# Second product accumulated on the first in one PSUM bank, one VectorE sum per block

## The chip, the cores and the metric

The kernel runs on one core of one Trainium2 chip. The metric is the device time of one execution in microseconds (us). Three runs of the kernel before gave 288.61, 289.20 and 290.28; their median is 289.2. A difference is told in us or in per cent of that median.

## What is computed

A WaveNet layer: a causal convolution of three taps with dilation 2, then tanh of one half of the channels times sigmoid of the other half, then a matrix product. `x` is 2 x 16000 x 256, `w` is 3 x 256 x 512, `w_o` is 256 x 256, all bf16.

```python
xp = jnp.pad(x, ((0, 0), (pad, 0), (0, 0)))          # pad = (K - 1) * dil = 4
h = jnp.einsum('btc,cd->btd', xp[:, pad:pad + T, :], w[0])
for i in range(1, K):
    off = pad - i * dil
    h = h + jnp.einsum('btc,cd->btd', xp[:, off:off + T, :], w[i])
z = jnp.tanh(h[..., :D]) * _sigmoid(h[..., D:])
return z @ w_o
```

So `h[t] = x[t] w0 + x[t-2] w1 + x[t-4] w2`.

## The kernel before

**Layout.** Time is split as t = 4r + j. The input arrives transposed in SBUF (tile `xt`: channels on the partitions, then j, channel half, r), by DMA transposes of the sync queue, except for the first 160 rows, which come as they are and are transposed on TensorE (`turn`). A group is 256 rows r (1024 time steps); each of the two sequences has 16 groups, the very first and the very last of 160 rows. 32 groups make 128 blocks: each group has four blocks, one for each 128 of the 512 columns of `h` (in the order 0, 2, 1, 3, so that a tanh block is followed by its sigmoid block).

**Two halves of time.** With xc = x at j = 0, 1, yc = x at j = 2, 3 and xp, yp the same one row earlier, a block needs

- for j = 0, 1: xc w0 + yp w1 + xp w2
- for j = 2, 3: yc w0 + xc w1 + yp w2

Done directly (`direct`, the first four blocks) this is 12 matmuls, six for each half (three taps, two channel halves). The other 124 blocks use four products in place of six, that is 8 matmuls of 512 columns (`products(k, which)`, L208 to L227):

- product 2: (xc - yp) times wm, wm = (w0 + w2 - w1) / 2
- product 1: (xc + yp) times wp, wp = (w0 + w2 + w1) / 2
- product 3: (yc - yp) times w0
- product 0: (xp - xc) times w2

Product 1 plus product 2 plus product 0 is the half j = 0, 1; product 1 minus product 2 plus product 3 is the half j = 2, 3.

**Before the change** product 2 goes into a PSUM bank "b" and product 1 into a bank "a". ScalarE copies b into SBUF (`copy_m2`, L254, tile `ss`). VectorE makes both sums in place (`combine`, L261: b = a - ss; L262: a = a + ss). Product 3 is then accumulated on b and product 0 on a, and ScalarE applies tanh or sigmoid to b and to a (`activate`, L275). VectorE multiplies tanh and sigmoid (`gate`, L284, tile `zz`); TensorE multiplies by w_o (`out_mm`, L295, four matmuls of 256 columns in a piece, four pieces in a group); ScalarE copies a piece to SBUF (`out_evict`, L309) and the sync queue stores it.

**Moving operands.** `m` = xc - yp (`pre_m`, L183) and `p` = xc + yp (`pre_p`, L189) are made by VectorE, the differences `d` of products 3 and 0 (`pre_d`, L200) by GpSimd, each a group ahead; for group 1 three of the four d's are VectorE's. The weights wm and wp are made by VectorE at the start (`weights`, L149 to L152).

**PSUM.** Eight banks: pool `ps_a` has three buffers, `ps_b` three, `ps_o` two. A buffer that is asked for anew waits for the last reader of its tile three allocations earlier (two for `ps_o`).

**Order.** The schedule is written by hand; each engine runs its instructions in the order of the program text. After the start the main loop has one step per block k:

- TensorE: products 2 and 1 of block k, products 3 and 0 of block k-1, one piece of output matmuls
- ScalarE: copy of block k, eviction of the last piece, activations of block k-1 (b, then a)
- VectorE: one of pre_m, gate, pre_p, gate; then the two sums of block k
- GpSimd: one d for the next group, held behind VectorE's operation

The start: a few warm-up matmuls on zeros (`warm_up`, L97) write into tiles of `ps_a`; then TensorE transposes and runs the direct blocks 0 and 1, tap by tap, then 2 and 3, with products 2 and 1 of block 4 set before the last tap of block 3. Meanwhile VectorE makes the weights, the first gate, m, p and three d's.

Of the kernel before, what the change touches and what calls it, by code (L numbers as in the profile page):

```python
# [9 lines left out]
ALU = mybir.AluOpType  # L10
# [3 lines left out]
def kernel(  # L14
# [18 lines left out]
    nc = tc.nc  # L33
    bf16 = mybir.dt.bfloat16
    f32 = mybir.dt.float32
    B, T, D = x.shape
    K, _, D2 = w.shape
    P = 128
    assert K == 3 and D % P == 0 and D2 == 2 * D and T % 64 == 0
    CT = D // P  # L40
    NT = D // P
    RH = 16
    RG = 256
# [5 lines left out]
    N_DIRECT = 4  # L49
# [15 lines left out]
    for b in range(B):  # L65
# [4 lines left out]
        while i < len(rs):  # L70
            n = cuts.pop(0) if cuts else 2
# [17 lines left out]
    ps_a = ctx.enter_context(tc.tile_pool(name="ps_a", bufs=3, space=bass.MemoryType.PSUM))  # L89
    ps_b = ctx.enter_context(tc.tile_pool(name="ps_b", bufs=3, space=bass.MemoryType.PSUM))  # L90
# [1 line left out]
    ctx.enter_context(tc.manual_schedule())  # L92

    def warm_up(n):
        wps = ps_a.tile([P, 2 * RG], f32, name="a")
        for _ in range(n):
            nc.tensor.matmul(  # L97
                wps[:], lhsT=warm[:, 0:P], rhs=warm[:, :],
                start=True, stop=True,
            )  # L100
# [24 lines left out]
    w_taps = [w0_sb, w12_sb[:, 0], w12_sb[:, 1]]  # L125
    nc.scalar.preload_act_table(ACT.Sigmoid)
    warm_up(N_WARM_A)
    xns = []
    for i, (r0, r) in enumerate(TILES):
        xn = consts.tile([P, 4, D], bf16, name=f"xn{i}")  # L130
        nc.sync.dma_start(
            out=xn[:r], in_=x[0, 4 * r0:4 * (r0 + r), :].rearrange("(r j) c -> r j c", j=4)
# [12 lines left out]
    wp_sb = consts.tile([P, CT, D2], bf16)  # L145
# [27 lines left out]
    def views(g):  # L173
        G = groups[g]
        xt, c, R = xts[G["chunk"]], RH + G["col"], G["R"]
        return (xt[:, 0:2, :, c - 1:c - 1 + R], xt[:, 2:4, :, c - 1:c - 1 + R],
                xt[:, 0:2, :, c:c + R], xt[:, 2:4, :, c:c + R])

    def pre_m(g):
        xp, yp, xc, yc = views(g)  # L180
        G = groups[g]
        G["m"] = m_pool.tile([P, 2, CT, RG], bf16, name="mm")
        return nc.vector.tensor_tensor(out=G["m"][:, :, :, :G["R"]], in0=xc, in1=yp, op=ALU.subtract)  # L183
# [7 lines left out]
    def pre_d(g, part, eng, behind=None):  # L191
        xp, yp, xc, yc = views(g)
        G = groups[g]
        R = G["R"]
        if "d" not in G:
            G["d"] = d_pool.tile([P, 4, CT, RG], bf16, name="dd")
        h, q = divmod(part, 2)
        a, s = (yc, yp) if h == 0 else (xp, xc)
        j = 2 + q if h == 0 else q
        ins = eng.tensor_tensor(out=G["d"][:, j, :, :R], in0=a[:, q], in1=s[:, q], op=ALU.subtract)  # L200
        if behind is not None:
            tc.add_manual_dep(
                ins.ins, behind.ins.name,
                mybir.DependencyInfo(mybir.DependencyClass.Sync, mybir.DependencyReason.DATA),
                reason="GpSimd reads SBUF while VectorE's sums read PSUM",
            )

    def products(k, which):  # L208
        g, oi = divmod(k, 4)
        G = groups[g]  # L210
        o = O_ORDER[oi]
        osl = slice(o * P, (o + 1) * P)
        R = G["R"]
        N = 2 * R
        if which in (1, 2):
            G["ab"[which - 1], oi] = (ps_a, ps_b)[which - 1].tile([P, 2 * RG], f32, name="ab"[which - 1])
        wmat, mv, bank, first = {
            2: (wm_sb, lambda ct: G["m"][:, :, ct, :R], "b", True),
            1: (wp_sb, lambda ct: G["p"][:, :, ct, :R], "a", True),
            3: (w_taps[0], lambda ct: G["d"][:, 2:4, ct, :R], "b", False),  # L220
            0: (w_taps[2], lambda ct: G["d"][:, 0:2, ct, :R], "a", False),
        }[which]
        for ct in range(CT):
            nc.tensor.matmul(  # L224
                G[bank, oi][:, :N], lhsT=wmat[:, ct, osl], rhs=mv(ct),
                start=first and ct == 0, stop=ct == CT - 1, skip_group_check=True,
            )  # L227

    def direct(k, taps):

        g, oi = divmod(k, 4)
        G = groups[g]
        o = O_ORDER[oi]
        osl = slice(o * P, (o + 1) * P)
        R = G["R"]
        xp, yp, xc, yc = views(g)
        for tap in taps:
            if tap == 0:
                G["a", oi] = ps_a.tile([P, 2 * RG], f32, name="a")
                G["b", oi] = ps_b.tile([P, 2 * RG], f32, name="b")  # L240
            for bank, mv in (("a", (xc, yp, xp)[tap]), ("b", (yc, xc, yp)[tap])):
                for ct in range(CT):
                    nc.tensor.matmul(  # L243
                        G[bank, oi][:, :2 * R], lhsT=w_taps[tap][:, ct, osl], rhs=mv[:, :, ct, :],
                        start=tap == 0 and ct == 0, stop=tap == K - 1 and ct == CT - 1,
                        skip_group_check=True,
                    )

    def copy_m2(k):
        g, oi = divmod(k, 4)  # L250
        G = groups[g]
        N = 2 * G["R"]
        G["ss", oi] = ss_pool.tile([P, 2 * RG], f32, name="ss")
        nc.scalar.copy(out=G["ss", oi][:, :N], in_=G["b", oi][:, :N])  # L254

    def combine(k):
        g, oi = divmod(k, 4)
        G = groups[g]
        N = 2 * G["R"]
        pa, pb, ss = G["a", oi], G["b", oi], G["ss", oi]  # L260
        nc.vector.tensor_tensor(out=pb[:, :N], in0=pa[:, :N], in1=ss[:, :N], op=ALU.subtract)  # L261
        nc.vector.tensor_tensor(out=pa[:, :N], in0=pa[:, :N], in1=ss[:, :N], op=ALU.add)  # L262

    def activate(k):
        g, oi = divmod(k, 4)
        G = groups[g]
        R = G["R"]
        o = O_ORDER[oi]
        if oi == 0:
            G["th"] = act_pool.tile([P, NT, 4, RG], bf16, name="th")  # L270
            G["sg"] = act_pool.tile([P, NT, 4, RG], bf16, name="sg")
            G["z"] = z_pool.tile([P, NT, 4, RG], bf16, name="zz")
        dst = G["th"][:, o] if o < NT else G["sg"][:, o - NT]
        for h, bank in ((1, "b"), (0, "a")):
            nc.scalar.activation(  # L275
                out=dst[:, 2 * h:2 * h + 2, :R],
                in_=G[bank, oi][:, :2 * R].rearrange("p (q r) -> p q r", q=2),
                func=ACT.Tanh if o < NT else ACT.Sigmoid,
            )

    def gate(g, dt):
        G = groups[g]
        R = G["R"]
        return nc.vector.tensor_tensor(  # L284
            out=G["z"][:, dt, :, :R], in0=G["th"][:, dt, :, :R], in1=G["sg"][:, dt, :, :R], op=ALU.mult
        )
# [30 lines left out]
    NG = len(groups)  # L317
    NB = 4 * NG
    todo, made = [], []
    turn(0)  # L320
    turn(1)
    warm_up(N_WARM_B)
    for tap in range(K):
        for k in range(2):
            direct(k, (tap,))
    weights()
    for k in range(2):
        activate(k)
# [5 lines left out]
    for part in range(3):  # L334
        last = pre_d(1, part, nc.vector)
    pre_d(1, 3, nc.gpsimd, last)

    direct(3, range(K - 1))
    products(N_DIRECT, 2)
    products(N_DIRECT, 1)  # L340
    copy_m2(N_DIRECT)
    direct(3, (K - 1,))
    activate(3)
    combine(N_DIRECT)
    pre_d(2, 0, nc.gpsimd, pre_m(2))

    k = N_DIRECT + 1
    while k < NB + 2 or todo or made:
        g, oi = divmod(k, 4)
        if k < NB:  # L350
            products(k, 2)
            products(k, 1)
            copy_m2(k)
        if k <= NB:
            products(k - 1, 3)
            products(k - 1, 0)

        for piece in made:
            out_evict(*piece, False)
        made = []  # L360
        n = 1 if k < NB else 2
        while todo and todo[0][0] <= k and n:
            piece = todo.pop(0)[1]
            out_mm(*piece)
            made.append(piece)
            n -= 1

        last = None
        if k < NB and oi in (0, 2) and g + 1 < NG:
            last = (pre_m if oi == 0 else pre_p)(g + 1)  # L370
        if oi == 3 and g < NG:
            last = gate(g, 0)
        if oi == 1 and 1 <= g <= NG:
            last = gate(g - 1, 1)
            G = groups[g - 1]
            for rb0 in range(0, G["R"], P):
                for jp in range(2):
                    todo.append((k + 1, (g - 1, rb0, jp)))
        if k < NB and g + 1 < NG:
            pre_d(g + 1, oi, nc.gpsimd, last)  # L380
        if k < NB:
            combine(k)
        if k <= NB:
            activate(k - 1)

        if k < NB and oi == 3 and loaded < len(chunks) and groups[min(g + 1, NG - 1)]["chunk"] + 2 >= loaded:
            load_chunk(loaded)
            loaded += 1
        k += 1
# [30 lines left out]
```

## Time and profile before

| | |
|---|---|
| three runs | 288.61, 289.20, 290.28 us (median 289.2) |
| span of the profiled execution, first to last instruction | 286.7 us |
| own time of the profiled execution | not listed; the median of the runs is 2.5 us above its span |
| granted TensorE clock, mean | 1.000 |
| TensorE matmuls (PE) | 280.3 us busy, 98% |
| TensorE weight loads (PEld) | 152.8 us, 53% |
| VectorE (DVE) | 245.2 us, 86% |
| ScalarE (ACT) | 261.0 us, 91% |
| GpSimd (POOL) | 126.3 us, 44% |
| VectorE sums, L261 and L262 | 124 each, mean 693 and 683 ns |
| ScalarE copy of product 2, L254 | 124, mean 580 ns |
| ScalarE activations, L275 | 256, mean 606 to 608 ns |
| ScalarE eviction, L309 | 128, mean 593 ns |

Busy time is the union of an engine's instructions; instructions that follow each other can overlap in the records, so the sum of their lengths can be larger than the busy time. Matmul ends are modelled: a matmul of 512 columns shows 377 ns on average, while the next one of a stream starts sooner than that. Rows of a timeline give the start from the beginning of the span, the length, the engine (an engine name with a q is its sequencer), the line, the operation, out<-in, the shape and the count of merged instructions; in brackets the idle time before it and what ended it.

### The profile page before, as it was taken

The numbers are of one execution on the slowest core, as the hardware profiler recorded it, in microseconds if no ns is written. First come the engines' busy times: TensorE is split into PE (matmuls) and PEld (weight loads), VectorE is DVE, ScalarE is ACT, GpSimd is POOL, SyncE is SP. The second block draws the span as 40 slices with busy tenths as digits, with TensorE's granted clock in tenths as the row PEclk, the third lists the DMA queues.
The fourth block names the chain that finished last, engine by engine and source line by source line (L and its number), as shares of the span: only waits on it lengthen the run. The fifth ranks groups of instructions, "written<-read, shape, count | busy, mean of one in ns | idle before, by whom it ended". The sixth has DMA issues, their size and how long they took to land.

```text
span 286.7 us, 4706 instructions
## 1 busy us (share of the span) xinstructions
PE 280.3 (98%) x1577; PEld 152.8 (53%) x1577; DVE 245.2 (86%) x384; ACT 261.0 (91%) x511; POOL 126.3 (44%) x129
## 2 busy tenths in 40 slices
PE   7999999999999999999999999999999999999994
PEld 3644555555555555555555555555555555555572
DVE  1998888898898988988988988988988988988860
ACT  2388999999999999999999999999999999999995
POOL 1254444454445445445445445445445545445300
PEclk9999999999999999999999999999999999999999
DMA  8991793561826427181361915428272351211213
GB/s 201 201 153 46 187 169 107 129 159 41 220 75 140 123 81 178 73 215 48 112 188 39 224 74 134 129 70 190 77 178 83 107 158 44 75 58 53 75 73 119
DMA packets 75463, 34.47 MB, mean 120 GB/s; under 512 B 66256, under 2 KB 67280, under 8 KB 75440
## 3 DMA queue, kind: packets, MB, share of 16 engines
q1 hardware_dynamic: 74640, 33.40, 44.7%
q10 hardware_dynamic: 800, 0.79, 0.9%
q8 instruction: 12, 0.20, 0.3%
q14 instruction: 11, 0.09, 0.1%
HBM read 1.25 MB, written 16.38 MB: 61 GB/s over the span
## 4 chain that ended last, share of the span: by engine, by line
PE 91%; DVE 3%; DMA 2%; ACT 2%; issue 0%; ACTq 0%
PE b L224 36%; PE a L224 36%; PE o_ps L295 19%; DMA w_sb<-in_w_dram 2%; ACT osb L309 1%; DVE zz L284 1%; DVE b L261 0%; DVE mm L183 0%; DVE wm_sb L152 0%; DVE wt_sb L150 0%; DVE wp_sb L152 0%; ACT sg L275 0%; DVE dd L200 0%; ACT th L275 0%; DVE pp L189 0%
## 5 line engine op out<-in xcount | busy, mean ns | idle before, releaser
L200 POOL TENSOR_TENSOR dd<-xt 128x512 bf16<-128x512 bf16 (+1 forms) x121 | 125.4, 1037 | 145.4 <-DVE zz L284 79.2
L261 DVE TENSOR_TENSOR b<-a,ss 128x512 f32<-128x512 f32 (+1 forms) x124 | 85.9, 693 | 17.2 <-ACT ss L254 16.5
L262 DVE TENSOR_TENSOR a<-a,ss 128x512 f32<-128x512 f32 (+1 forms) x124 | 84.7, 683 | 0.0
L254 ACT COPY ss<-b 128x512 f32<-128x512 f32 (+1 forms) x124 | 72.0, 580 | 13.7 <-PE b L224 1.7
L224 PEld LDWEIGHTS <-w_sb 128*128 128x128 bf16 x496 | 48.5, 98 | 57.9 <-issue 1.3
L295 PE MATMUL o_ps<-wo_sb,zz 128*128 128x256 bf16 (+1 forms) x512 | 76.5, 273 | 0.7 <-ACT osb L309 0.7
L309 ACT CAST osb<-o_ps 128x512 bf16<-128x512 f32 (+1 forms) x128 | 75.5, 593 | 0.5 <-ACT osb L309 0.5
L224 PE MATMUL b<-mm,wm_sb 128*128 128x512 bf16 (+1 forms) x248 | 73.2, 377 | 0.1
L224 PE MATMUL b<-dd,w_sb 128*128 128x512 bf16 (+1 forms) x248 | 73.1, 377 | 0.1
L224 PE MATMUL a<-pp,wp_sb 128*128 128x512 bf16 (+1 forms) x248 | 73.2, 377 | 0.0
L224 PE MATMUL a<-dd,w_sb 128*128 128x512 bf16 (+1 forms) x248 | 73.2, 377 | 0.0
L295 PEld LDWEIGHTS <-zz 128*128 128x128 bf16 (+1 forms) x512 | 49.8, 98 | 33.0 <-PE b L224 0.8
L284 DVE TENSOR_TENSOR zz<-th,sg 128x1024 bf16<-128x1024 bf16 (+1 forms) x64 | 44.3, 691 | 12.6 <-ACT sg L275 12.4
L275 ACT ACTIVATE th<-b 128x512 bf16<-128x512 f32 (+1 forms) x64 | 38.8, 606 | 3.8 <-PE b L243 3.7
L275 ACT ACTIVATE sg<-b 128x512 bf16<-128x512 f32 (+1 forms) x64 | 38.9, 607 | 1.0 <-PE b L243 0.6
L224 PEld LDWEIGHTS <-wp_sb 128*128 128x128 bf16 x248 | 24.2, 98 | 28.9 <-DVE pp L189 0.5
L275 ACT ACTIVATE sg<-a 128x512 bf16<-128x512 f32 (+1 forms) x64 | 38.9, 608 | 0.0
L275 ACT ACTIVATE th<-a 128x512 bf16<-128x512 f32 (+1 forms) x64 | 38.8, 606 | 0.0
L224 PEld LDWEIGHTS <-wm_sb 128*128 128x128 bf16 x248 | 24.0, 98 | 3.9 <-DVE mm L183 0.5
L189 DVE TENSOR_TENSOR pp<-xt 128x1024 bf16<-128x1024 bf16 (+1 forms) x31 | 21.8, 702 | 0.0
L183 DVE TENSOR_TENSOR mm<-xt 128x1024 bf16<-128x1024 bf16 (+1 forms) x31 | 21.1, 680 | 0.0
L243 PEld LDWEIGHTS <-w_sb 128*128 128x128 bf16 x48 | 4.7, 97 | 2.2
(22 smaller groups left out, 26.0 us busy)
## 6 DMA issues: line engine op xcount, KB each, us to landing
out_dram<-osb SPq DMA_DIRECT2D x62, 256.0 KB, 2.0
w_sb<-in_w_dram ACTq DMA_DIRECT2D x1, 512.0 KB, 5.5
xn<-in_x_dram SPq DMA_DIRECT2D x2, 160.0 KB, 3.7
w_sb<-in_w_dram ACTq DMA_DIRECT2D x1, 256.0 KB, 4.0
xt<-in_x_dram SPq DMA_TRANSPOSE x16, 6.5
wo_sb<-in_w_o_dram SPq DMA_DIRECT2D x1, 128.0 KB, 5.5
out_dram<-osb SPq DMA_DIRECT2D x2, 64.0 KB, 1.6
```

The lines of the kernel that those rows point to most:

```text
L183: return nc.vector.tensor_tensor(out=G["m"][:, :, :, :G["R"]], in0=xc, in1=yp, op=ALU.subtract)
L189: return nc.vector.tensor_tensor(out=G["p"][:, :, :, :G["R"]], in0=xc, in1=yp, op=ALU.add)
L200: ins = eng.tensor_tensor(out=G["d"][:, j, :, :R], in0=a[:, q], in1=s[:, q], op=ALU.subtract)
L224: nc.tensor.matmul(G[bank, oi][:, :N], lhsT=wmat[:, ct, osl], rhs=mv(ct), start=first and ct == 0, stop=ct == CT - 1, skip_group_check=True,)
L243: nc.tensor.matmul(G[bank, oi][:, :2 * R], lhsT=w_taps[tap][:, ct, osl], rhs=mv[:, :, ct, :], start=tap == 0 and ct == 0, stop=tap == K - ...
L254: nc.scalar.copy(out=G["ss", oi][:, :N], in_=G["b", oi][:, :N])
L261: nc.vector.tensor_tensor(out=pb[:, :N], in0=pa[:, :N], in1=ss[:, :N], op=ALU.subtract)
L262: nc.vector.tensor_tensor(out=pa[:, :N], in0=pa[:, :N], in1=ss[:, :N], op=ALU.add)
L275: nc.scalar.activation(out=dst[:, 2 * h:2 * h + 2, :R], in_=G[bank, oi][:, :2 * R].rearrange("p (q r) -> p q r", q=2), func=ACT.Tanh if o ...
L284: return nc.vector.tensor_tensor(out=G["z"][:, dt, :, :R], in0=G["th"][:, dt, :, :R], in1=G["sg"][:, dt, :, :R], op=ALU.mult)
L295: nc.tensor.matmul(o_ps[:rn, q, :], lhsT=G["z"][:, dt, 2 * jp + q, rb0:rb0 + rn], rhs=wo_sb[:, dt, :], start=(dt == 0), stop=(dt == NT - 1),)
L309: nc.scalar.copy(out=osb[:rn, 2 * jp:2 * jp + 2, :], in_=o_ps[:rn])
```

## The change

Product 1 is accumulated on top of product 2 in bank b, after ScalarE has copied product 2 out of it. Bank b then holds the sum of the two. One VectorE instruction (`scalar_tensor_tensor`) writes bank a = b - 2 ss, which is product 1 minus product 2. Product 0 is accumulated on b and product 3 on a, so that the halves change places: b now is j = 0, 1 and a is j = 2, 3.

Since product 1 has to follow the copy, the loop is one step deeper. In step k TensorE runs product 2 of block k, product 1 of block k-1, products 0 and 3 of block k-2, then the output piece; ScalarE evicts the last piece first, then copies block k and activates block k-2; VectorE has its bf16 operation (pre_m and pre_p now in the second and fourth step of a group, the gates in the third and first) and the one sum, that of block k-1. Bank b is taken in step k and released by the activation in step k+2; bank a is taken at the sum.

No matmul starts bank a any more with the flag that clears it. So the warm-up matmuls go over all three buffers of `ps_a`, and in the four direct blocks VectorE sets the a bank to zero first (L243 of the changed kernel), after which the matmuls of the taps accumulate on it, b ahead of a in each tap. In the text of the program the memset of block 2 stands behind `weights()`, and that of block 3 behind the first gate, pre_m, pre_p and the three d's of group 1. Product 1 of block 4 moves from the start into the loop; `pre_m(2)` is issued twice, once ahead of the loop and once in its first step.

```diff
--- before.py
+++ after.py
@@ -92,8 +92,10 @@
     ctx.enter_context(tc.manual_schedule())
 
     def warm_up(n):
-        wps = ps_a.tile([P, 2 * RG], f32, name="a")
-        for _ in range(n):
+
+        for t in range(n):
+            if t % 2 == 0:
+                wps = ps_a.tile([P, 2 * RG], f32, name="a")
             nc.tensor.matmul(
                 wps[:], lhsT=warm[:, 0:P], rhs=warm[:, :],
                 start=True, stop=True,
@@ -212,13 +214,13 @@
         osl = slice(o * P, (o + 1) * P)
         R = G["R"]
         N = 2 * R
-        if which in (1, 2):
-            G["ab"[which - 1], oi] = (ps_a, ps_b)[which - 1].tile([P, 2 * RG], f32, name="ab"[which - 1])
+        if which == 2:
+            G["b", oi] = ps_b.tile([P, 2 * RG], f32, name="b")
         wmat, mv, bank, first = {
             2: (wm_sb, lambda ct: G["m"][:, :, ct, :R], "b", True),
-            1: (wp_sb, lambda ct: G["p"][:, :, ct, :R], "a", True),
-            3: (w_taps[0], lambda ct: G["d"][:, 2:4, ct, :R], "b", False),
-            0: (w_taps[2], lambda ct: G["d"][:, 0:2, ct, :R], "a", False),
+            1: (wp_sb, lambda ct: G["p"][:, :, ct, :R], "b", False),
+            0: (w_taps[2], lambda ct: G["d"][:, 0:2, ct, :R], "b", False),
+            3: (w_taps[0], lambda ct: G["d"][:, 2:4, ct, :R], "a", False),
         }[which]
         for ct in range(CT):
             nc.tensor.matmul(
@@ -238,11 +240,12 @@
             if tap == 0:
                 G["a", oi] = ps_a.tile([P, 2 * RG], f32, name="a")
                 G["b", oi] = ps_b.tile([P, 2 * RG], f32, name="b")
-            for bank, mv in (("a", (xc, yp, xp)[tap]), ("b", (yc, xc, yp)[tap])):
+                nc.vector.memset(G["a", oi][:, :2 * R], 0.0)
+            for bank, mv in (("b", (xc, yp, xp)[tap]), ("a", (yc, xc, yp)[tap])):
                 for ct in range(CT):
                     nc.tensor.matmul(
                         G[bank, oi][:, :2 * R], lhsT=w_taps[tap][:, ct, osl], rhs=mv[:, :, ct, :],
-                        start=tap == 0 and ct == 0, stop=tap == K - 1 and ct == CT - 1,
+                        start=bank == "b" and tap == 0 and ct == 0, stop=tap == K - 1 and ct == CT - 1,
                         skip_group_check=True,
                     )
 
@@ -254,12 +257,15 @@
         nc.scalar.copy(out=G["ss", oi][:, :N], in_=G["b", oi][:, :N])
 
     def combine(k):
+
         g, oi = divmod(k, 4)
         G = groups[g]
         N = 2 * G["R"]
-        pa, pb, ss = G["a", oi], G["b", oi], G["ss", oi]
-        nc.vector.tensor_tensor(out=pb[:, :N], in0=pa[:, :N], in1=ss[:, :N], op=ALU.subtract)
-        nc.vector.tensor_tensor(out=pa[:, :N], in0=pa[:, :N], in1=ss[:, :N], op=ALU.add)
+        G["a", oi] = ps_a.tile([P, 2 * RG], f32, name="a")
+        nc.vector.scalar_tensor_tensor(
+            out=G["a", oi][:, :N], in0=G["ss", oi][:, :N], scalar=-2.0, in1=G["b", oi][:, :N],
+            op0=ALU.mult, op1=ALU.add,
+        )
 
     def activate(k):
         g, oi = divmod(k, 4)
@@ -271,7 +277,7 @@
             G["sg"] = act_pool.tile([P, NT, 4, RG], bf16, name="sg")
             G["z"] = z_pool.tile([P, NT, 4, RG], bf16, name="zz")
         dst = G["th"][:, o] if o < NT else G["sg"][:, o - NT]
-        for h, bank in ((1, "b"), (0, "a")):
+        for h, bank in ((0, "b"), (1, "a")):
             nc.scalar.activation(
                 out=dst[:, 2 * h:2 * h + 2, :R],
                 in_=G[bank, oi][:, :2 * R].rearrange("p (q r) -> p q r", q=2),
@@ -337,28 +343,29 @@
 
     direct(3, range(K - 1))
     products(N_DIRECT, 2)
-    products(N_DIRECT, 1)
     copy_m2(N_DIRECT)
     direct(3, (K - 1,))
     activate(3)
-    combine(N_DIRECT)
     pre_d(2, 0, nc.gpsimd, pre_m(2))
 
     k = N_DIRECT + 1
-    while k < NB + 2 or todo or made:
-        g, oi = divmod(k, 4)
-        if k < NB:
-            products(k, 2)
-            products(k, 1)
-            copy_m2(k)
-        if k <= NB:
-            products(k - 1, 3)
-            products(k - 1, 0)
-
+    made = []
+    while k < NB + 3 or todo or made:
+        g, oi = divmod(k, 4)
         for piece in made:
             out_evict(*piece, False)
         made = []
-        n = 1 if k < NB else 2
+        if k < NB:
+            products(k, 2)
+        if N_DIRECT <= k - 1 < NB:
+            products(k - 1, 1)
+        if k < NB:
+            copy_m2(k)
+        if N_DIRECT <= k - 2 < NB:
+            products(k - 2, 0)
+            products(k - 2, 3)
+
+        n = 1 if k <= NB else 2
         while todo and todo[0][0] <= k and n:
             piece = todo.pop(0)[1]
             out_mm(*piece)
@@ -366,22 +373,22 @@
             n -= 1
 
         last = None
-        if k < NB and oi in (0, 2) and g + 1 < NG:
-            last = (pre_m if oi == 0 else pre_p)(g + 1)
-        if oi == 3 and g < NG:
-            last = gate(g, 0)
-        if oi == 1 and 1 <= g <= NG:
+        if k < NB and oi in (1, 3) and g + 1 < NG:
+            last = (pre_m if oi == 1 else pre_p)(g + 1)
+        if oi == 2 and g >= 1 and g - 1 < NG:
             last = gate(g - 1, 1)
             G = groups[g - 1]
             for rb0 in range(0, G["R"], P):
                 for jp in range(2):
                     todo.append((k + 1, (g - 1, rb0, jp)))
+        if oi == 0 and 2 <= g <= NG:
+            last = gate(g - 1, 0)
         if k < NB and g + 1 < NG:
             pre_d(g + 1, oi, nc.gpsimd, last)
-        if k < NB:
-            combine(k)
-        if k <= NB:
-            activate(k - 1)
+        if N_DIRECT <= k - 1 < NB:
+            combine(k - 1)
+        if N_DIRECT <= k - 2 < NB:
+            activate(k - 2)
 
         if k < NB and oi == 3 and loaded < len(chunks) and groups[min(g + 1, NG - 1)]["chunk"] + 2 >= loaded:
             load_chunk(loaded)
```

## The prediction

> **What bounds it now.** I read the profile's page first: its span line, its busy shares and the slices.
>
> ```profile
> span 286.7 us, 4706 instructions
> ...
> PE 280.3 (98%) x1577; PEld 152.8 (53%) x1577; DVE 245.2 (86%) x384; ACT 261.0 (91%) x511; POOL 126.3 (44%) x129
> ...
> PE   7999999999999999999999999999999999999994
> ```
>
> PE is busy 98% of the span; only the first and the last slice have holes. Busy is not the same as at its peak, so I went on to the timeline of one block in the middle (columns: start, length, engine, line, what).
>
> ```profile
> 153.35 0.59 PE L224 MATMUL b<-mm,wm_sb 128*128 128x512 bf16 x2
> ...
> 153.79 0.59 PE L224 MATMUL a<-pp,wp_sb 128*128 128x512 bf16 x2
> ...
> 154.03 0.58 ACT L254 COPY ss<-b 128x512 f32<-128x512 f32 x1
> 154.22 0.59 PE L224 MATMUL b<-dd,w_sb 128*128 128x512 bf16 x2
> 154.51 0.59 ACT L309 CAST osb<-o_ps 128x512 bf16<-128x512 f32 x1
> ...
> 154.65 0.59 PE L224 MATMUL a<-dd,w_sb 128*128 128x512 bf16 x2
> ...
> 154.99 0.62 ACT L275 ACTIVATE th<-b 128x512 bf16<-128x512 f32 x1
> 155.08 0.60 PE L295 MATMUL o_ps<-wo_sb,zz 128*128 128x256 bf16 x4
> ...
> 155.48 0.62 ACT L275 ACTIVATE th<-a 128x512 bf16<-128x512 f32 x1
> 155.52 0.38 PE L224 MATMUL b<-mm,wm_sb 128*128 128x512 bf16 x1
> ```
>
> The pairs start 0.43 apart, so one matmul of 512 columns goes in every 0.216; the four output matmuls take 0.44. A block is 8 x 0.216 + 0.44 = 2.16, which is what lies between the two b<-mm rows (153.35 to 155.52). So PE is fed without a gap, and nothing that VectorE or ScalarE saves can shorten a block. ScalarE's four instructions start 0.48 to 0.49 apart, 1.95 of the 2.16; VectorE (two sums of 0.70 and 0.69, and one bf16 operation of 0.69) has some room too. What can move is the start, the end, and any new wait inside a block.
>
> The start (timeline, VectorE's chain and PE's first wait):
>
> ```profile
> 9.50 1.22 DVE L152 SCALAR_TENSOR_TENSOR wp_sb<-wt_sb,wh_sb 128x1024 bf16<-128x1024 f32 x1
> ...
> 10.70 1.26 DVE L284 TENSOR_TENSOR zz<-th,sg 128x640 bf16<-128x640 bf16 x1
> ...
> 11.88 0.68 DVE L183 TENSOR_TENSOR mm<-xt 128x1024 bf16<-128x1024 bf16 x1
> ...
> 12.62 0.60 PE L224 MATMUL b<-mm,wm_sb 128*128 128x512 bf16 x2
> ```
>
> Here VectorE has no pause from 6.76 on, and PE waits for it: direct blocks 2 and 3 are PE's filler while VectorE makes the weights, m, p and d.
>
> **The change, part by part.**
>
> *Steady blocks, work.* PE's eight products and four output matmuls stay: 0. VectorE loses one sum of 0.69 a block: PE doesn't wait for it in the middle of the run, so 0. The new instruction is not in the trace with these operands; L261 (a plain sum of the same three tiles) takes 0.70, and half of L152 (the same operation over 1024 elements, 1.22) is 0.61. I take 0.70. It has from the end of product 1 (1.04 into its block) to product 0 of the next step (2.16 + 0.86 = 3.03), behind one bf16 operation of 0.69 at most, so twice that length would still be hidden.
>
> *Steady blocks, the new waits.* Product 1 of block k now waits for ScalarE's copy of block k, a whole step earlier: nearly 1.3 to spare. The tight one is bank b. It is now held from product 2 in step k to the activation in step k+2, and the pool has three: product 2 of step k+3 waits for the activation that reads b in step k+2. Behind that matmul stands the whole PE queue. From the start of a step: products 2 and 1, 4 x 0.216 = 0.86; from the start of the pair of product 0 to an idle ScalarE's activation 0.63, and that activation 0.60:
>
> ```profile
> 17.05 0.59 PE L224 MATMUL b<-dd,w_sb 128*128 128x512 bf16 x2
> ...
> 17.68 0.60 ACT L275 ACTIVATE sg<-b 128x512 bf16<-128x512 f32 x1 [0.40 <-PE b L224]
> ```
>
> and from the end of a ScalarE instruction to a matmul that waits for it 0.05 (near the end an osb copy of 0.66 at 280.30 ends at 280.96, and o_ps starts at 281.01). Sum 0.86 + 0.63 + 0.60 + 0.05 = 2.14 against 2.16: free 0.02 before it is needed. ScalarE is idle at that point: the osb copy and the ss copy that stand before the activation end 1.37 into the step, and product 0 ends at 1.46. So I cost this at 0, with almost no cover. The other end: an activation of 0.62, as in the middle of the run, and a wake-up of 0.68, that of the ss copy, which waits for several semaphores (18.52 to 19.20), give 2.21, 0.05 late in each of some 116 blocks, 5.8 in all. The activation waits for PE alone, as the 17.68 row does, so I take that row.
>
> *The start.* Each of the four direct blocks gets a VectorE memset of its a bank, and the a matmuls wait for it. A memset of 128x320 in PSUM is not in the trace: the memset of warm (256 elements in SBUF) takes 0.27, a sum over 320 in PSUM 0.49; I take 0.35, a memset with 64 elements more. The first two run at 6.0 and 6.3, before VectorE's weights (which wait for their DMA until 6.76), and are done when PE needs them (6.58 and 7.12): 0. The third stands behind wp: it can start at 10.7, ends at 11.05, PE sees it at 11.1. PE has by then done block 2's first pair of b (now 9.59 to 9.86) and stands: 1.2 lost. Five pairs of 0.27 and b's first pair of block 3 bring it to 12.74. The fourth memset stands behind the gate, m, p and three d. The gate took a slot of 1.19 (10.70 to 11.88) with GpSimd's d beside it until 11.6; the same gate alone took 0.41 (15.91 to 16.32). It now starts at 11.0, so I take 0.8 (both ends for the range). From m to after the d's it is 11.88 to 14.11 = 2.23. So the memset starts at 11.0 + 0.8 + 2.2 = 14.0, PE sees it at 14.4: 1.65 lost. Three pairs more (0.82), product 2 of block 4 (0.43) and the last tap (0.55): product 2 of block 5 starts at 16.2, in place of 14.23. That is 1.97 late, and product 1 of block 4 (0.43), done by then before, is still owed: +2.4. With memsets of 0.27 and a gate of 0.41 it is +1.8, with 0.49 and 1.19 it is +3.0.
>
> *The filling of the pipeline.* From product 2 of block 5 to that of block 8, PE lost 0.69 before: 20.97 - 14.23 = 6.74 against three steps of work (1.73 + 2.16 + 2.16). With one sum in place of two those waits go. What is late next: product 1 of block 5 waits for its copy, which is behind two activations of block 3 (0.18), and product 2 of block 7 for bank b of block 4, in a step that has no output matmuls beside it (0.41). Sum 0.59: -0.1.
>
> *The end.* One more step, but one sum less in the last chain: copy, product 1, sum, products 0 and 3, activations, gate. Laid out by the rows of 277 to 281, PE stands 0.6 before the last group's output matmuls; it stood 0.68 (280.33 to 281.01): -0.1.
>
> Sum: +2.4 + 0 - 0.1 - 0.1 = **+2.2** on the span of 286.7, so 288.9. Around the span lie 2.5 us, if the profiled execution stands at the median of the three runs (289.2, from 288.61 to 290.28); it has no time of its own in the listing. Forecast **291.4**, and 290.8 to 292.0 by the ends of the start.
>
> **Where a rule speaks against the change.** The six warm-up matmuls at 1.19 took 2.74, 0.43 each; the three at 5.66 took 0.81 in all, 0.216 apart. So PE's first matmuls ran at half pace, while the PEclk row shows 9 throughout. Between 3.93 and 5.66 PE had only two transposes of under 0.5 and kept the full pace behind them. The new holes (1.2 and 1.65) are of that size. The Trainium skill, "TensorE: Matmul & The Clock Gate", "A second HAM failure mode: psum-queue depth-cycling", says that short idle times between groups of matmuls, while PSUM banks are cycled, can throw PE back to half its clock. By that rule the holes would cost a further stretch at half pace; the trace here speaks against it (full pace right after PE's waits at 12.1 to 13.2).
>
> **The rivals.**
> 1. *Bank b is late* (18%). If ScalarE's wake-up or its length is over the 0.02 to spare, each block gets longer: 0.025 x 116 = 2.9 on top, 294.3; up to 297.2. For it: the margin is 1% of a block. Against it: the one row that has this very wait gives 0.63 and 0.60.
> 2. *Half pace after the holes* (5%). One stretch as at the start (six matmuls, 0.43 in place of 0.216) or somewhat more costs 1.3 to 1.7: 293.
> 3. *Not slower* (13%). VectorE's chain in the start decides. If the gate runs in 0.41, since the memset ahead of it leaves GpSimd's d time to finish, the memsets take 0.27, and the filling loses nothing, then +1.8 - 0.69 - 0.1 = +1.0: 290.2, within 0.5%. The end of the fourth memset counts one for one (14.35 is the +2.4 above): at 13.6 the whole is +1.45 with the filling as I have it, at 14.3 with a filling that loses nothing; before that it is this rival.
> 4. *Faster* (2%). All of PE's waits in the start and filling (0.28, 0.18, 0.69) would have to go and the memsets cost nothing: -1.1, 288.1, still within 0.5%; only a chance of the measurement makes it more. That the change does not do what it says would be a DVE count that does not fall by about 120; its order of instructions has one sum a block.
>
> **How the numbers follow.** The forecast holds 62%. A difference of 0.5% (1.4 us) is about what the measurement tells from none. "Same" is rival 3 and 5 of the forecast's 62 points, for runs that come out low: 0.18; faster 0.02; slower 0.80. The range goes from rival 3's time to the middle of rival 1: 290.2 to 294.6.
>
> **What would show it.** Right: PE holes of 1.2 and 1.65 in the first 15 us, ended by memsets of L243; then b<-mm rows 2.16 apart with PE at 9 in every slice; ACT idle about 0.1 before each activation of b. Wrong: b<-mm rows 2.18 or more apart, waits of PE b for ACT th or sg in the list of waits; matmuls 0.43 apart after a hole; the fourth memset done before 13.6.

## The result, and the profile after

The changed kernel took **291.85 us** (median of nine runs, 290.90 to 292.21). The kernel before, run beside it, took 289.71 (nine runs, 288.61 to 290.43). The ratio is 1.0074, with a 95% interval from 1.0055 to 1.0094: slower. The difference of the medians is 2.14; the forecast was +2.2 and 291.4. The profiled spans differ by 2.7 (289.4 against 286.7).

The page of the changed kernel: span, busy shares, PE's slices, and two groups (count, busy time and mean length in ns, idle time before them and what ended it).

```profile
span 289.4 us, 4582 instructions
...
PE 280.0 (97%) x1577; PEld 152.9 (53%) x1577; DVE 198.2 (68%) x265; ACT 260.0 (90%) x511; POOL 127.0 (44%) x129
...
PE   7689999999999999999999999999999999999994
...
L265 DVE SCALAR_TENSOR_TENSOR a<-ss,b 128x512 f32<-128x512 f32 (+1 forms) x124 | 85.5, 690 | 31.0 <-PE b L226 30.0
```

The change did what it says: VectorE has 119 instructions fewer and is busy for 47 us less, and the new sum takes 0.69, as the plain one did. PE's work is the same (280.0). From the fourth slice on PE's row is that of before, 9 in all but the last. What is new stands in slices two and three (6 and 8 where before there were nines), the first 22 us.

The timeline there (start, length, engine, line, what; in brackets the idle time before and what ended it):

```profile
7.08 0.43 DVE L151 TENSOR_SCALAR wh_sb<-w_sb 128x1024 bf16<-128x1024 bf16 x1 [0.32 <-DMA w_sb<-in_w_dram]
...
9.59 0.43 PE L246 MATMUL b<-xt,w_sb 128*128 128x320 bf16 x2
...
9.82 1.22 DVE L154 SCALAR_TENSOR_TENSOR wp_sb<-wt_sb,wh_sb 128x1024 bf16<-128x1024 f32 x1
...
11.10 0.33 DVE L243 MEMSET a<- 128x320 f32 x1
11.34 0.95 DVE L290 TENSOR_TENSOR zz<-th,sg 128x640 bf16<-128x640 bf16 x1
11.48 0.43 PE L246 MATMUL a<-xt,w_sb 128*128 128x320 bf16 x2 [1.46 <-DVE a L243]
...
11.75 0.44 PE L246 MATMUL b<-xt,w_sb 128*128 128x320 bf16 x2
...
12.21 0.68 DVE L185 TENSOR_TENSOR mm<-xt 128x1024 bf16<-128x1024 bf16 x1
...
12.85 0.43 PE L246 MATMUL b<-xt,w_sb 128*128 128x320 bf16 x2
...
13.42 1.09 DVE L202 TENSOR_TENSOR dd<-xt 128x512 bf16<-128x512 bf16 x3
14.57 0.33 DVE L243 MEMSET a<- 128x320 f32 x1
...
14.96 0.44 PE L246 MATMUL a<-xt,w_sb 128*128 128x320 bf16 x2 [1.67 <-DVE a L243]
...
16.77 0.59 PE L226 MATMUL b<-mm,wm_sb 128*128 128x512 bf16 x2
```

These are the two holes that were forecast, and each ends with a memset. The bracket counts from the modelled end of the last matmul. Counted in PE's own rhythm, the pair of b at 9.59 is through at 9.86 (pairs of 320 columns are 0.27 apart), so the first hole is 11.48 - 9.86 = 1.62. The second, from 13.12 (the pair at 12.85 and 0.27) to 14.96, is 1.84. Behind each hole the pairs are again 0.27 apart.

A block in the middle:

```profile
152.15 0.59 ACT L281 ACTIVATE sg<-a 128x512 bf16<-128x512 f32 x1
...
152.33 0.59 PE L226 MATMUL b<-mm,wm_sb 128*128 128x512 bf16 x2
...
152.76 0.59 PE L226 MATMUL b<-pp,wp_sb 128*128 128x512 bf16 x2
...
153.19 0.59 PE L226 MATMUL b<-dd,w_sb 128*128 128x512 bf16 x2
...
153.82 0.60 ACT L281 ACTIVATE th<-b 128x512 bf16<-128x512 f32 x1
...
154.49 0.38 PE L226 MATMUL b<-mm,wm_sb 128*128 128x512 bf16 x1
```

Product 2 is again 2.16 apart (152.33 to 154.49). The activation that frees the bank taken at 154.49 is the one at 153.82. To the nanosecond it ends at 154.420, and the matmul starts at 154.491: 0.07 later, where 0.05 is needed. So 0.02 is to spare, and no wait shows. It is so in every block of the middle: the distance is 0.070 to 0.072, and ScalarE stands 0.11 before these activations (0.1 was forecast). From product 2 of block 12 to that of block 122 both kernels take 237.967 us.

### The profile page after: what moved, and what is told of

The parts are those of the page before. It is cut to its first block, busy times and chain, and to the rows that moved or that the text cites. A ratio compares the mean times of both kernels' runs of the same rounds, so it can differ in the third digit from the quotient of the medians.

```text
span 289.4 us, 4582 instructions
## 1 busy us (share of the span) xinstructions
PE 280.0 (97%) x1577; PEld 152.9 (53%) x1577; DVE 198.2 (68%) x265; ACT 260.0 (90%) x511; POOL 127.0 (44%) x129
## 4 chain that ended last, share of the span: by engine, by line
PE 91%; DVE 3%; ACT 3%; DMA 2%; issue 0%; ACTq 0%
PE b L226 54%; PE o_ps L301 18%; PE a L226 18%; DMA w_sb<-in_w_dram 2%; ACT osb L315 1%; ACT th L281 1%; DVE wm_sb L154 0%; DVE wt_sb L152 0%; DVE wp_sb L154 0%; ACT sg L281 0%; DVE dd L202 0%; PE a L246 0%; DVE zz L290 0%; ACT ss L257 0%; DVE a L243 0%
## 5 line engine op out<-in xcount | busy, mean ns | idle before, releaser
L265 DVE SCALAR_TENSOR_TENSOR a<-ss,b 128x512 f32<-128x512 f32 (+1 forms) x124 | 85.5, 690 | 31.0 <-PE b L226 30.0
L257 ACT COPY ss<-b 128x512 f32<-128x512 f32 (+1 forms) x124 | 75.6, 610 | 3.2 <-PE b L226 3.1
L226 PE MATMUL b<-pp,wp_sb 128*128 128x512 bf16 (+1 forms) x248 | 73.1, 376 | 0.0
L281 ACT ACTIVATE th<-b 128x512 bf16<-128x512 f32 (+1 forms) x64 | 37.6, 588 | 12.1 <-PE b L246 5.1
L281 ACT ACTIVATE sg<-b 128x512 bf16<-128x512 f32 (+1 forms) x64 | 37.6, 587 | 6.8 <-PE b L226 0.6
L185 DVE TENSOR_TENSOR mm<-xt 128x1024 bf16<-128x1024 bf16 (+1 forms) x32 | 37.9, 1185 | 0.0
L281 ACT ACTIVATE th<-a 128x512 bf16<-128x512 f32 (+1 forms) x64 | 37.2, 582 | 0.0
L281 ACT ACTIVATE sg<-a 128x512 bf16<-128x512 f32 (+1 forms) x64 | 37.2, 582 | 0.0
L191 DVE TENSOR_TENSOR pp<-xt 128x1024 bf16<-128x1024 bf16 (+1 forms) x31 | 34.3, 1106 | 0.0
L246 PE MATMUL a<-xt,w_sb 128*128 128x320 bf16 x24 | 5.2, 299 | 3.1 <-DVE a L243 3.1
```

What stands on the lines that cost most here:

```text
L191: return nc.vector.tensor_tensor(out=G["p"][:, :, :, :G["R"]], in0=xc, in1=yp, op=ALU.add)
L226: nc.tensor.matmul(G[bank, oi][:, :N], lhsT=wmat[:, ct, osl], rhs=mv(ct), start=first and ct == 0, stop=ct == CT - 1, skip_group_check=True,)
L246: nc.tensor.matmul(G[bank, oi][:, :2 * R], lhsT=w_taps[tap][:, ct, osl], rhs=mv[:, :, ct, :], start=bank == "b" and tap == 0 and ct == 0, ...
L265: nc.vector.scalar_tensor_tensor(out=G["a", oi][:, :N], in0=G["ss", oi][:, :N], scalar=-2.0, in1=G["b", oi][:, :N], op0=ALU.mult, op1=ALU.add,
L281: nc.scalar.activation(out=dst[:, 2 * h:2 * h + 2, :R], in_=G[bank, oi][:, :2 * R].rearrange("p (q r) -> p q r", q=2), func=ACT.Tanh if o ...
```

## The experiments

Kernels under one heading ran on one chip and share the runs of the kernel before that the heading names; under the last heading they are named for each.

### Do the memsets hold all of the cost?

The kernel before, in these runs: 289.66 (29 runs).

**Memsets early.** The memset of block 2 stands ahead of the weights, that of block 3 right behind them.

```diff
+    zero(2)
     weights()
     for k in range(2):
         activate(k)
+    zero(3)
...
-                G["a", oi] = ps_a.tile([P, 2 * RG], f32, name="a")
+                if k < 2:
+                    zero(k)
                 G["b", oi] = ps_b.tile([P, 2 * RG], f32, name="b")
-                nc.vector.memset(G["a", oi][:, :2 * R], 0.0)
```

> The changed kernel with the last two memsets moved ahead on VectorE: that of block 2 ahead of the weights, that of block 3 right behind them, ahead of the first gate. My theory (the loss is TensorE standing for these two memsets): both holes of 1.5 and 1.7 us close, product 2 of block 5 starts near 14.0 in place of 16.8; some 0.6 is given back, since VectorE's two pre_m(2) then delay the first sum. About 1.6 us less than the changed kernel, 290.2 against 289.7 before. Rivals: if bank b costs time in each block, or the deeper pipeline does, the time stays near 291.9; if TensorE's pace falls behind the holes, more than 2.2 us come back.

Measured: 290.22, ratio 1.0026 [1.0008, 1.0044], span 288.2. The time is as expected, and neither hole is there: PE's pairs run 0.27 apart from 8.66 to 13.60. Before that they ran at half pace in this execution (more on this below), so product 2 of block 5 starts at 15.03, not near 14.0. The same four memsets, placed elsewhere in VectorE's order, cost 0.26% in place of 0.74%.

**No memset.** The direct blocks use the tiles that the warm-up matmuls have filled with zeros; for block 3 one more warm-up matmul makes such a tile.

```diff
-                G["a", oi] = ps_a.tile([P, 2 * RG], f32, name="a")
+                if k == 3:
+                    warm_up(1)
+                G["a", oi] = zeros[k + 2]
                 G["b", oi] = ps_b.tile([P, 2 * RG], f32, name="b")
-                nc.vector.memset(G["a", oi][:, :2 * R], 0.0)
```

> The changed kernel without any memset in the direct blocks: they take the tiles that the warm-up matmuls (zeros times zeros) have left at zero, and block 3 gets one more warm-up matmul of 512 columns (0.22 on TensorE). My theory: no TensorE wait for VectorE before product 2 of block 4, which starts near 12.6 as in the kernel before; product 2 of block 5 near 13.6; the doubled pre_m(2) then holds the first sum back by 0.6. About 289.9, 2 us less than the changed kernel. Rival (a loss in each block, or in the deeper pipeline): near 291.9.

Measured: 290.07, ratio 1.0004 [0.9983, 1.0025]. The time is as expected: without memsets the rest of the change (one sum, the deeper loop, bank b held longer) can't be told from nothing. The starts were not as expected: PE ran at half pace up to about 9.9 in this execution too, and product 2 of block 5 is at 15.77, not near 13.6. The runs of both kernels come in two kinds (also below), and each kind agrees: three of the 12 runs here lie from 288.70 to 288.79 and the rest from 289.36 to 290.61; of the 29 of the kernel before ten lie from 288.43 to 288.87 and the rest from 289.50 to 290.63.

**No memset, and one `pre_m(2)`.** As before this one, with the doubled bf16 operation issued once.

```diff
-    pre_d(2, 0, nc.gpsimd, pre_m(2))
+    pre_d(2, 0, nc.gpsimd, last)
```

> As the kernel without memsets, and pre_m(2) issued once, in the loop. My theory: the first sum starts when product 1 of block 4 is done, product 0 of block 4 does not wait, another 0.6 us less: about 289.3, 0.4 below the kernel before. Rival: the second pre_m is hidden, and the time is that of the kernel without memsets.

Measured: 289.80, ratio 1.0010 [0.9992, 1.0029]: a miss by 0.5, and the rival holds. The second `pre_m` was not the cost that I took it for. In the profile of the kernel without memsets VectorE stands before the first sum and waits for PE, so the second `pre_m` is hidden there:

```profile
16.91 0.70 DVE L269 SCALAR_TENSOR_TENSOR a<-ss,b 128x512 f32<-128x512 f32 x1 [0.30 <-PE b L229]
```

With one `pre_m(2)` the sum starts at 16.89, no earlier. PE ran at half pace up to about 9.9 in both executions; no trace of these two kernels shows the sum with the full pace early.

**The kernel before with memsets.** The memsets, the order b ahead of a and the warm-up over three buffers, and nothing else of the change.

```diff
             if tap == 0:
...
+                nc.vector.memset(G["a", oi][:, :2 * R], 0.0)
-            for bank, mv in (("a", (xc, yp, xp)[tap]), ("b", (yc, xc, yp)[tap])):
+            for bank, mv in (("b", (yc, xc, yp)[tap]), ("a", (xc, yp, xp)[tap])):
...
-                        start=tap == 0 and ct == 0, stop=tap == K - 1 and ct == CT - 1,
+                        start=bank == "b" and tap == 0 and ct == 0, stop=tap == K - 1 and ct == CT - 1,
```

> The kernel before with one part of the change alone: the four memsets in the direct blocks, with the a bank not cleared by its first matmul, b ahead of a in each tap, and the warm-up over all three buffers. My theory: the same two holes of 1.5 and 1.7 us, from which the 0.7 us goes off that TensorE waited for VectorE's sums while the pipeline filled: +2.1, about 291.8. Rival (the loss lies in the accumulation on one bank, the bank's longer hold or the extra step): 289.7, as before.

Measured: 292.17, ratio 1.0083 [1.0060, 1.0105]. As expected: the memsets alone bring the whole cost. It is 2.5 here, but the intervals of the two ratios overlap, so whether it is more than that of the change is not shown. Its timeline:

```profile
12.09 0.33 DVE L242 MEMSET a<- 128x320 f32 x1
...
12.46 0.43 PE L245 MATMUL a<-xt,w_sb 128*128 128x320 bf16 x2
...
15.52 0.33 DVE L242 MEMSET a<- 128x320 f32 x1
...
15.90 0.45 PE L245 MATMUL a<-xt,w_sb 128*128 128x320 bf16 x2 [1.64 <-DVE a L242]
```

The second hole is that of the changed kernel (1.64, and 1.67 there). The first is small here: in this execution PE's first matmuls ran at half pace (below) and got to the memset so much later.

### Is bank b really 0.02 from being a wait?

The kernel before: 289.87 (11 runs).

**Four buffers for b.** `ps_a` has two buffers, `ps_b` four; nothing else.

> The changed kernel with four buffers for bank b and two for bank a. My theory: bank b is free 0.02 us before it is needed in the steady blocks, so a fourth buffer saves nothing there; it takes away the one wait of 0.4 us for bank b of block 4 while the pipeline fills: about 291.5. Rival (the bank's longer hold costs something in each block): 1 to 3 us less, at 290.5 or below.

Measured: 291.82, ratio 1.0066 [1.0044, 1.0088], and 2.163 a block as before. As expected: there was no wait in the steady blocks for the fourth bank to take away. In the filling there was one: in the changed kernel product 2 of block 7 has [0.25 <-ACT th L281] and starts 2.32 behind product 2 of block 6 (17.63 to 19.95); here it is 1.90 (17.50 to 19.40). Those 0.42 are about as much as the 0.41 of the prediction. In the changed kernel:

```profile
17.63 0.59 PE L226 MATMUL b<-mm,wm_sb 128*128 128x512 bf16 x2
...
19.95 0.59 PE L226 MATMUL b<-mm,wm_sb 128*128 128x512 bf16 x2 [0.25 <-ACT th L281]
```

Little of the 0.42 shows in the time. A part is paid back at the start: with two buffers for a, the first memset waits for the warm-up matmuls (it starts at 6.39 in place of 6.10) and holds PE up by 0.2.

**Product 3 ahead of product 0.** Two lines of the changed kernel trade places, so that the activation of b comes 0.43 later; all work is the same.

```diff
-            products(k - 2, 0)
             products(k - 2, 3)
+            products(k - 2, 0)
```

> The changed kernel with product 3 ahead of product 0 in each step, so that bank b is read 0.43 us later. My theory (the sum 0.63 + 0.60 + 0.05 from the start of product 0's pair to the matmul that takes the bank): product 0's pair starts 1.30 into the step, so a step takes 1.30 + 1.28 = 2.58 in place of 2.16, +0.41 in some 116 blocks: 48 us more, about 339. Rival (the wait for the bank has more room than I counted): a step of 2.16 to 2.4.

Measured: **340.69** (two runs), ratio 1.176 [1.172, 1.180], and 2.57 a block. The theory gave 339 and 2.58. Its timeline in the middle:

```profile
151.30 0.59 PE L226 MATMUL b<-mm,wm_sb 128*128 128x512 bf16 x2 [0.25 <-ACT sg L281]
...
152.59 0.59 PE L226 MATMUL b<-dd,w_sb 128*128 128x512 bf16 x2
...
153.23 0.60 ACT L281 ACTIVATE th<-b 128x512 bf16<-128x512 f32 x1 [0.52 <-PE b L226]
...
153.88 0.59 PE L226 MATMUL b<-mm,wm_sb 128*128 128x512 bf16 x2 [0.25 <-ACT th L281]
```

Here the chain can be read off: product 0 starts 1.29 behind product 2 (three products), the activation 0.64 later, it lasts 0.60, and 0.05 behind its end the next product 2 starts. These are the terms of the prediction with a product more: 2.58.

**The same with four buffers for b** (both edits).

> Product 3 ahead of product 0, and four buffers for bank b, two for bank a. My theory: the wait for bank b alone makes the order of the two products matter; with a fourth buffer the step is 2.16 again and the time about 291.5, that of four buffers in the changed order. Rival (something else than the bank is late, such as ScalarE's order): well above 300.

Measured: 292.13, ratio 1.0083 [1.0053, 1.0113], 2.163 a block. The fourth bank takes all of the 49 us back, so they were the wait for bank b and nothing else. It came out 0.6 above the number expected. Its four runs lie from 291.40 to 292.58; in the profiled one the second transposes start 0.33 later than in the profile before, at 5.69, and the first memset holds PE up by 0.2, as it does with four buffers alone. Whether the transposes are late in all its runs is not settled.

### Why do runs of the kernel before come in two kinds?

The 24 runs of the kernel before under this heading are split: 11 from 288.37 to 288.85, 13 from 289.44 to 290.70, none between (median 289.49). The profiles of the memset experiments showed PE at half pace up to 8.4 to 10 us, while that of the kernel before had it only for the first six matmuls.

**The kernel before once more**, unchanged: the profile of another execution.

> The kernel before once more, one look. If this execution is one of the slower ones (289.5 to 290.6), its profile should show the three warm-up matmuls at 5.7 and the first direct matmuls at half pace, and a span near 288.3 in place of 286.7; if it is one of the faster ones, full pace from 5.7 on and a span of 286.7.

Measured: 290.05, span 288.3. PE's rows from the trace of the first profiled execution of the kernel before:

```profile
5.66 0.81 PE L97 MATMUL a<-warm 128*128 128x512 bf16 x3
6.31 0.43 PE L243 MATMUL a<-xt,w_sb 128*128 128x320 bf16 x2
6.58 0.44 PE L243 MATMUL b<-xt,w_sb 128*128 128x320 bf16 x2
```

and from this one:

```profile
5.65 1.48 PE L97 MATMUL a<-warm 128*128 128x512 bf16 x3
6.92 0.74 PE L243 MATMUL a<-xt,w_sb 128*128 128x320 bf16 x2
7.46 0.74 PE L243 MATMUL b<-xt,w_sb 128*128 128x320 bf16 x2
```

Same program, same moment, pairs 0.27 apart in the one and 0.54 in the other, until 9.60. The granted-clock row shows 9 in every slice of both. The spans are 286.7 and 288.3: the kind of an execution is the moment at which PE goes to full pace. In the traces of this case without further warm-up matmuls that is between 3.7 and 5.7 us, or between 8.4 and 10.2. The Trainium skill, "TensorE: Matmul & The Clock Gate", "What's actually happening", describes half the clock until a free-running window of 3.4 us has been busy, and a change that moves by 0.5 us from run to run. The half pace agrees with the traces (0.54 against 0.27), and the 0.5 us does not: the change comes before 5.7 in one kind and after 8.4 in the other. By the Trainium skill's window, as an estimate, a window that holds the pause and so doesn't count as busy would put the change 3.4 us later; no run here shows the window itself.

**Two warm-up matmuls between the two transposes**, where PE had stood for 0.78.

```diff
     turn(0)
+    warm_up(2)
     turn(1)
```

In the kernel before:

> The kernel before with two more warm-up matmuls between the two sets of transposes at the start. In the profiles so far TensorE takes the first direct matmuls either at full pace from 5.7 us on (this kernel, the changed one) or at half pace up to 8.4 to 10 us (the kernels with early or no memsets, the memsets alone). My theory: that is what splits the runs of the kernel before into 288.4 to 288.9 and 289.5 to 290.6; with TensorE busy between the transposes the full pace comes early each time, and all runs lie at 288.4 to 288.9. Rival (the split has another cause, a DMA of the start): the runs stay split.

In the changed kernel:

> The changed kernel with the same two warm-up matmuls. My theory: with the pace settled the holes alone make the difference, 1.6 + 1.8 us of them less what the filling gives back: 2.7 above the kernel before with the same warm-up, near 291.2. Rival (half pace in the start is part of the loss): less than 2 above it.

Measured: 288.68 (12 runs, 288.42 to 289.18; ratio to before 0.9977 [0.9958, 0.9995]) and 291.51 (7 runs, 291.22 to 292.45; 1.0074 [1.0046, 1.0102]). Both near what was expected. The upper kind is gone from the 12 runs (nine are at 288.87 or below, and three from 288.99 to 289.18, between the two kinds), so it is the pause between the transposes that lets the full pace come so late. Why, with the pause, it comes at the one moment or the other is not shown. With the pace held in both, the change costs 291.51 - 288.68 = 2.83.

### A version that is faster than both

**No memset, warm-up between the transposes**: no memset and one `pre_m(2)` as under the first heading, `warm_up(2)` as above, and `zeros[k + 3]` for `zeros[k + 2]`, since the two new matmuls take a tile more (the kernel before: 289.49).

> The changed kernel without memsets, pre_m(2) issued once, and the same two warm-up matmuls. My theory: product 2 of block 5 starts near 13.6, and the lighter VectorE gives 0.3 to 0.5 in the filling and at the end: 288.2, lowest of all, 0.4 below the kernel before with the same warm-up. Rival (the change in itself costs something in the start): 289 or more.

Measured: 289.05, ratio 0.9992 [0.9971, 1.0013]: a miss by 0.85. Its timeline shows where that went:

```profile
14.16 1.13 POOL L205 TENSOR_TENSOR dd<-xt 128x512 bf16<-128x512 bf16 x1 [2.35 <-DMA xt<-in_x_dram]
...
14.31 1.52 DVE L188 TENSOR_TENSOR mm<-xt 128x1024 bf16<-128x1024 bf16 x1
...
15.76 0.68 DVE L269 SCALAR_TENSOR_TENSOR a<-ss,b 128x512 f32<-128x512 f32 x1
...
16.50 0.61 PE L229 MATMUL b<-dd,w_sb 128*128 128x512 bf16 x2 [0.52 <-DVE a L269]
```

`pre_m(2)`, 0.68 by itself, takes 1.52 beside GpSimd's d, and the first sum, which PE needs, stands behind it.

On this chip three kernels have the two warm-up matmuls: the kernel before (288.68), the changed one (291.51) and this one. So of the 2.83 that the change costs with the pace held, the memsets and the second `pre_m(2)` hold 2.46, and 0.37 are left. What holds these is not shown; the further warm-up matmul of block 3 takes 0.22, and PE's wait for the first sum is the last row above.

**The sum of block 4 first**: `combine(4)` ahead of `pre_m(2)`, and GpSimd's first d for group 2 behind it (the kernel before: 290.11).

```diff
+        if k == N_DIRECT + 1:
+            combine(k - 1)
         last = None
...
+        if k == N_DIRECT + 1:
+            pre_d(g + 1, 0, nc.gpsimd, last)
```

> The changed kernel without memsets and with the two more warm-up matmuls, as in the last run, but the sum of block 4 stands ahead of pre_m(2) on VectorE, and GpSimd's first d of group 2 behind it. There pre_m(2) took 1.52 beside GpSimd's d, and product 0 of block 4 waited 0.52 for the sum. My theory: that wait goes, the sum of block 4 starts about 0.1 after product 1; 0.5 less than 289.05, 288.5, about level with the kernel before with the same warm-up (288.68). Rival: another wait for VectorE or GpSimd takes its place, and the time stays at 289.

Measured: **288.35** (6 runs, 287.96 to 289.13), ratio 0.9942 [0.9921, 0.9962]. As expected. PE's wait in the place of the last fence is gone:

```profile
15.57 0.70 DVE L269 SCALAR_TENSOR_TENSOR a<-ss,b 128x512 f32<-128x512 f32 x1 [1.22 <-PE b L229]
...
16.17 0.69 DVE L188 TENSOR_TENSOR mm<-xt 128x1024 bf16<-128x1024 bf16 x1
...
16.32 0.61 PE L229 MATMUL b<-dd,w_sb 128*128 128x512 bf16 x2
```

It is the lowest of all, 0.6% below the kernel before. But 10 of the 11 runs of the kernel before on that chip were of the upper kind; the one of the lower kind took 288.51, and the kernel before with the two warm-up matmuls 288.68 on another chip. From these the version can't be told. So it beats both kernels as they stand, and whether anything of its gain is the second product's place, and not PE's pace at the start, is not settled.

## Why the prediction was right, step by step

- **Steady work, 0: right.** 47 us less of VectorE's time changed no block: 2.163 before and after. The sum of 0.70 measured 0.69.
- **Bank b, 0.02 to spare: right, and the margin was as thin as worked out.** 0.07 between the end of the activation and the matmul in each block, 0.05 needed. A shift of 0.43 in PE's order turned it into 0.41 a block; the fourth bank removed that and brought nothing without the shift.
- **The start, +2.4: right in its mechanism, mis-sized.** Product 2 of block 5 starts at 16.77, against 14.23 before; with the 0.43 still owed that is +2.97. The holes are 1.62 and 1.84 in place of 1.2 and 1.65. Four terms were too small: the weights' transfer let VectorE start at 7.08 in place of 6.76 in this execution (0.3); the third memset began only when wp had ended (11.04 to 11.10), where I had let it overlap; the gate took a slot of 0.87, not 0.8; and from m to the fourth memset it was 2.36 (12.21 to 14.57), not 2.2, since that memset too waited for the d's to end. Less 0.06 (the gate followed the third memset after 0.24, not 0.3) these are the 0.6. The memset itself was 0.33 (taken 0.35).
- **The filling, -0.1: right.** From product 2 of block 5 to that of block 8 it took 22.11 - 16.77 = 5.34; the prediction's terms give 5.35.
- **The end, -0.1: right.** Before the last output group PE stands 0.57 (0.6 forecast, 0.68 before).
- **From span to time, 2.5 us: too large.** The changed kernel's profiled run has a span of 289.4 and a time of 291.31, 1.9 more, and a run of the kernel before with a span of 286.7 took 288.53. The 2.5 set a span of the lower kind against a median over both kinds. So 0.6 too little in the start and 0.6 too much around the span cancelled in that execution (291.31, forecast 291.4). That is luck.
- **The base.** The profiled execution of before was of the lower of its two kinds. Medians over both kinds give 2.14 for the change, the profiles 2.7, and with the pace held it is 2.83. The prediction's 2.2 agrees with the first by luck: it knew of one kind only. That the medians lie closer together has a reason in the trace of the kernel before with memsets, though in this one alone: when the full pace comes late, PE gets to the third memset later and stands 0.29 (12.17 to 12.46), not 1.62, so a kernel with memsets loses less by the late pace.
- **The rival of half pace behind the holes: did not occur.** The prediction's ground for that was weaker than it looked: the pause after which it saw full pace was followed by half pace up to 9.6 in the other execution of the same kernel. What settles it are the rows here. The pairs are 0.27 apart right behind both, and in the experiment with product 3 first PE waits 0.41 in every block and keeps 0.216 a matmul. The Trainium skill's "A second HAM failure mode: psum-queue depth-cycling" isn't borne out by this case's waits, though all of them cycle PSUM banks. The rival "not slower" needed a fourth memset that is done before 13.6; it ended at 14.90.

## What to carry to other kernels

Taking instructions off an engine that was not the bound gained nothing here, but an instruction put into its queue that the bound waits for can cost its whole place in that queue: here a memset of 0.33 us, behind 3.2 us of other work, cost PE 1.8 us. Ask of such a set-up instruction whether it can stand at the very front, or whether another engine's work already leaves the value behind. And work out how long each buffer is held in a step against the step itself, since a kernel that runs with 0.02 us to spare looks free of waits until two lines trade places and cost 17%.

## What the runs showed of the hardware

- PE was at full pace by 5.4 us in one execution and only behind 9.6 in another of the same program, which has a pause of 0.7 to 0.8 us in its warm-up, and the spans differ by 1.6 of 287; the granted-clock row doesn't show it, only the spacing of the matmuls does. With two matmuls in the pause none of the 12 runs was of the upper kind; the latest full pace in a trace with them is at about 7 us (the last kernel above).
- VectorE's operations on two SBUF inputs stretch beside a GpSimd one and stretch it too: `pre_m` 0.68 alone and 1.52 beside a d, the first gate 0.95 beside a d that takes 2.12 in place of 1.04. The sum with one input in PSUM kept its 0.69. The Trainium skill, "SBUF — State Buffer", "Who interferes with whom", has the two block each other for the length of an instruction; the rows come near it: the d of 14.16 ends at 15.29, and a `pre_m` started then would end at 15.97, 0.14 later than it did (15.83).
